# Three charges of a planner and its table of decisions, in a two-layer transformer kernel

## The chip, the cores and the metric

The kernel runs on one core of one Trainium2 chip. The metric is the device time of one execution in microseconds; a figure of the kernel before is the median of three executions. One further execution was recorded by the hardware profiler, and all views of the trace come from it.

The core's engines work beside each other and wait for each other by semaphores: PE multiplies matrices into PSUM, ACT evaluates functions (here the exponential), DVE and POOL do elementwise work, and SP issues the DMA transfers. POOL can't read PSUM.

## The reference

```python
def _A_ref(x, wqkv, wo):                    # attention: H = 32 heads of 16
    qkv = (x @ wqkv).reshape(B, S, 3, H, Dh).transpose(2, 0, 3, 1, 4)
    q, k, v = qkv[0], qkv[1], qkv[2]
    scores = jnp.einsum("bhqd,bhkd->bhqk", q, k) * (Dh ** -0.5)
    p = _softmax(scores, axis=-1)
    o = jnp.einsum("bhqk,bhkd->bhqd", p, v)
    return o.transpose(0, 2, 1, 3).reshape(B, S, D) @ wo
def _B_ref(x, w1, w2):                      # a dense layer with relu
    return jnp.maximum(x @ w1, 0) @ w2

x = A_x                                     # S = 2048 rows of D = 512, bf16
x = x + _A_ref(_layernorm(x), A_wqkv, A_wo)
x = x + _B_ref(_layernorm(x), B_w1, B_w2)   # 1792 hidden columns
x = x + _A_ref(_layernorm(x), A_wqkv, A_wo) # the same weights again
x = x + _B_ref(_layernorm(x), B_w1, B_w2)
return x
```

Two layers, each with 32 heads of 2048 x 2048 scores: 2 x 32 x 2048 x 2048 exponentials, 268 million, are the bulk of the work outside the matmuls.

## The kernel before

**Blocks and slots.** The scores of one head are cut into blocks of 128 keys by 512 queries (256 or 128 queries near the end of the second layer). A *slot* takes three such blocks of different heads: one group of score matmuls (L2231) fills one of two PSUM areas `ps_s`, three banks wide, and one ACT instruction (L2249) takes the exponential of what lies there into a buffer in SBUF. There are 1366 slots. The score matmuls of different heads run side by side in row groups of the array.

**Long and short exponentials.** In most slots the third block isn't given to ACT. DVE reads it from PSUM (`dve_block`, L1750), scales it and writes 16-bit integers, whose bits read as bf16 are a piecewise linear approximation of the exponential; POOL makes two shifted copies of it with integer additions (L1811), one up, one down. The three "words" together, with the lowest one weighed by `WEIGHT`, give a better approximation. So such a block costs PE three matmuls with the values instead of one. Two such blocks make a pair, which shares the words' buffers. The exponential of ACT then has 1024 columns and is called short here; with all three blocks it has 1536 and is long. The buffers for exponentials and words are few: three wide ones, 16 tiles of words, and whatever other tensors lie idle at the time and are lent (x, weights, keys, values).

**Weighing.** The lower word is weighed in one of two ways: if the values of those keys are at hand multiplied by `WEIGHT` (`vscaled`), the matmul takes these; otherwise DVE multiplies the word itself (`weigh` in `chain`, L1816).

**Values and filler.** The matmuls with the values (L1404) sum the output of one head group over all keys in one of two PSUM banks, `ps_o` and `ps_f`. Four of them run side by side in column groups of the array; such a round of four is called a pass here. Between the score groups PE also does the *filler*: the projections to queries, keys and values, the output projection, and both matmuls of the dense layer (L467, L707, L716), in pieces of a pass. The filler's sums go to that one of the two banks which the values don't hold, and DVE copies them out.

**Norms and transposes.** For a group of (mostly) four times 128 rows DVE computes statistics, ACT the inverse root, DVE the normalized rows (`ln_apply`, L795), and SP issues a DMA transpose for each 128 rows (L846) into `xnT`, from which the next filler is computed.

**The order.** Nothing is scheduled at run time. The program is written out slot by slot by a planner in the kernel's source: it keeps a clock for each engine (`now_pe`, `now_dve`, `now_act`, `now_pool`, `sp_free`), adds a charge in ns for everything it issues, and marks when each result will be there. For each slot it decides from these clocks whether a pair starts, which passes of values and filler go ahead of the next score group, and in which order DVE and POOL take their tasks. Each engine then runs its instructions in the order in which they were written, and the semaphores make it wait where a result isn't there. The charges of this change stand in `TRANSPOSE` (SP's time for an issue, then the time until the data is there), in the task of `apply` in `ln_rows`, and in `quick` in `chain`.

Two tables steer the decisions. `RULES` sets parameters from a slot on (how many passes may go ahead, how far a pair may look, how much backlog DVE may have). `STARTS`, `MORE` and `SLIP` override single slots: a pair starts or doesn't, more or less filler is owed, the limit for passes moves by some ns. They are read at these places:

```python
rule.update(RULES.get(no, {}))
asked = STARTS.get(no)
owed[0] = min(owed[0] + pace, rule["cap"]) + MORE.get(no, 0) if todo else 0.0
limit = max(need_by - rule["margin"], s_ready) - SWITCH + SLIP.get(no, 0.0)
```

When too many exponentials lie unread, or no buffer is free for the next one, the planner issues passes with values after the slot's scores (`force_v`), and the exponential has to wait until they have read the buffer that it writes.

The head (until the first exponential) and the end (after the last) are written out by hand, and neither the charges nor the tables change them.

Of the kernel before, what the change touches and what calls it, by code (L numbers as in the profile page):

```python
# [26 lines left out]
def kernel(  # L27
# [24 lines left out]
    QS = 512  # L52
# [18 lines left out]
    GROUP = 2  # L71
# [14 lines left out]
    EVAC_V, BESIDE, TUCK = 661.0, 10.0, {512: 0.0, 256: 11.0, 128: 24.0}  # L86
    STREAMED, WINDOW = 0.56, 3413.0
    SPREAD_LAG = 5000.0
    SMALL, W1, TRANSPOSE = (600.0, 1600.0), (430.0, 3000.0), (1400.0, 3600.0)
    CROWDED, POOL_ISSUE, BEHIND = 4500.0, 700.0, 3500.0  # L90
    JOINING, ADDED, BEHIND_IT = 870.0, 4300.0, 300.0
    JOIN = {}
    LOADED, FIRST_LOAD, LATER_LOAD, KEPT_Q = 18000.0, 30, 180, 8
    BOTH = 4
    WHOLE = 4
    STARTS, MORE, SLIP = {13: 0, 16: 1, 40: 0, 23: 1, 30: 0, 33: 0, 56: 0, 53: 0, 54: 1, 47: 0, 103: 1, 127: 1, 141: 1, 184: 1, 252: 1, 254: 0, 313: 0, 342: 0, 353: 0, 344: 1, 370: 1, 382: 1, 419: 1, 451: 0, 453: 1, 456: 0, 444: 0, 508: 0, 509: 1, 538: 0, 532: 1, 547: 0, 566: 1, 578: 0, 585: 1, 592: 0, 642: 1, 654: 0, 646: 0, 641: 1, 670: 0, 696: 1, 682: 0, 719: 0, 715: 1, 728: 1, 737: 1, 772: 0, 819: 1, 834: 0, 857: 0, 844: 1, 855: 0, 854: 1, 873: 0, 886: 1, 905: 1, 918: 1, 938: 1, 929: 0, 976: 0, 1000: 0, 1006: 1, 1001: 0, 1025: 0, 1031: 1, 1092: 0, 1128: 1, 1151: 1, 1166: 1, 1172: 0, 1250: 0, 1260: 0, 1266: 1, 1263: 0, 1340: 0, 1326: 0, 1364: 0, 1362: 0, 1366: 0, 1371: 0}, {9: -1.0, 13: 2.0, 7: 2.0, 38: 1.0, 39: 2.0, 32: 2.0, 52: 2.0, 41: -1.0, 48: 1.0, 126: 1.0, 153: 2.0, 187: -1.0, 204: 2.0, 221: -1.0, 237: 1.0, 229: -1.0, 264: 2.0, 265: -1.0, 266: 1.0, 300: 2.0, 281: 1.0, 285: 1.0, 308: 1.0, 320: 2.0, 318: -1.0, 327: -1.0, 355: 2.0, 378: -1.0, 371: 1.0, 372: 2.0, 388: 2.0, 396: -1.0, 391: -1.0, 437: 1.0, 495: 2.0, 538: 2.0, 543: 2.0, 574: 2.0, 603: 2.0, 659: 1.0, 684: -1.0, 685: 1.0, 711: -1.0, 807: 1.0, 804: 2.0, 813: -1.0, 828: 1.0, 836: 2.0, 832: 2.0, 855: 2.0, 879: 2.0, 861: -1.0, 862: -1.0, 896: 1.0, 897: 1.0, 899: 2.0, 956: -1.0, 948: 1.0, 961: 2.0, 987: -1.0, 1008: 1.0, 1035: -1.0, 1079: 1.0, 1089: 1.0, 1100: -1.0, 1099: -1.0, 1110: 2.0, 1164: 1.0, 1263: -1.0, 1267: 2.0, 1277: 2.0, 1299: 1.0, 1336: 2.0, 1365: -1.0, 1375: 1.0, 1371: 2.0}, {3: 120.0, 56: -200.0, 102: 60.0, 133: -200.0, 175: -200.0, 194: 120.0, 184: -200.0, 196: 120.0, 259: 60.0, 245: 60.0, 241: -200.0, 321: -200.0, 325: -200.0, 322: 60.0, 357: -200.0, 370: -200.0, 366: 120.0, 377: -200.0, 384: -200.0, 385: -200.0, 390: 120.0, 419: 120.0, 434: 216.0, 436: 120.0, 435: 60.0, 497: -200.0, 517: 60.0, 523: 60.0, 530: -200.0, 521: -200.0, 551: -200.0, 549: 60.0, 559: 216.0, 574: -200.0, 634: 60.0, 666: -200.0, 691: 216.0, 692: 60.0, 689: -200.0, 718: -200.0, 722: -200.0, 726: -200.0, 740: 120.0, 818: 120.0, 828: 60.0, 825: 60.0, 822: -200.0, 891: -200.0, 922: 60.0, 932: -200.0, 931: 120.0, 946: 60.0, 951: -200.0, 945: 60.0, 1011: 216.0, 1013: -200.0, 1002: 216.0, 1034: 60.0, 1062: 216.0, 1064: 120.0, 1067: 60.0, 1097: 60.0, 1114: 60.0, 1131: 120.0, 1220: -200.0, 1218: 60.0, 1242: 216.0, 1279: 60.0, 1289: -200.0, 1294: 216.0, 1296: 216.0, 1312: 60.0, 1307: -200.0, 1308: 60.0, 1323: 216.0, 1353: -200.0, 1361: -200.0, 1365: -200.0, 1370: -200.0}
    FIXED = 3
    rule = {
        "near": 14, "hold": 3, "spare": 14, "easy": 1.6, "cap": 6.0, "least": 0.5, "pace": 1.0,
# [2 lines left out]
        "rounds": 4, "partial": 3, "far": 3, "young": 3, "old": 5, "slack": 1300.0, "eager": 0,  # L102
        "haste": 2.0, "margin": 130.0, "join": -1.0, "room": 0, "keep": 2, "wide": 1, "share": 4,
    }
    RULES = {1: {'rounds': 3, 'hold': 2, 'closing': 3, 'fill': 2000.0}, 21: {'young': 5}, 41: {'easy': 1.0, 'keep': 1}, 61: {'old': 3, 'spare': 6, 'rounds': 4, 'fill': 3000.0, 'over': 200.0, 'young': 6, 'pressed': 6, 'closing': 6}, 101: {'least': 0.5, 'spare': 20, 'margin': 160.0, 'far': 4}, 121: {'near': 8, 'pressed': 2, 'soon': 1400.0, 'old': 4}, 141: {'keep': 2, 'late': 4.0, 'ahead': 8.0, 'unit': 360.0}, 161: {'pressed': 6, 'hold': 3, 'spare': 6, 'least': 0.8, 'far': 4, 'soon': 2000.0, 'haste': 1.6, 'near': 4}, 181: {'wide': 1, 'haste': 3.0}, 201: {'hold': 4, 'backlog': 3000.0}, 221: {'keep': 3, 'easy': 1.4, 'haste': 2.0, 'far': 2}, 241: {'haste': 3.0, 'full': 4}, 261: {'margin': 100.0}, 281: {'late': 3.0}, 301: {'late': 99.0, 'least': 0.5, 'unit': 400.0, 'easy': 1.0, 'keep': 2, 'young': 5, 'pace': 1.0, 'full': 3}, 321: {'keep': 3, 'easy': 2.0}, 341: {'young': 3}, 361: {'haste': 2.0}, 401: {'young': 6, 'unit': 360.0}, 421: {'pace': 1.0, 'slack': 1300.0, 'over': 0.0, 'eager': 0, 'partial': 3, 'backlog': 2200.0, 'closing': 3, 'cap': 3.0}, 441: {'pace': 1.15, 'young': 6, 'rounds': 4, 'keep': 2, 'calm': 3.0, 'far': 2, 'soon': 1400.0, 'unit': 320.0}, 461: {'slack': 1300.0, 'fill': 2000.0, 'closing': 3, 'unit': 360.0}, 481: {'unit': 400.0, 'soon': 2000.0, 'rounds': 4, 'late': 4.0, 'eager': 0, 'least': 0.5, 'fill': 2000.0, 'haste': 1.6}, 541: {'late': 2.0, 'least': 0.8}, 561: {'keep': 2, 'near': 10, 'margin': 100.0, 'hold': 2}, 581: {'ahead': 12.0, 'closing': 6, 'slack': 800.0, 'full': 5}, 601: {'ahead': 8.0, 'cap': 6.0}, 661: {'near': 12, 'ahead': 12.0, 'closing': 3, 'pace': 1.15}, 701: {'spare': 10}, 721: {'haste': 2.0, 'rounds': 4, 'near': 10, 'over': 0.0, 'pace': 1.3, 'eager': 1, 'keep': 2, 'young': 5}, 761: {'hold': 4, 'partial': 3, 'pace': 0.7, 'cap': 3.0, 'closing': 0, 'wide': 2, 'join': -1.0, 'near': 10}, 801: {'late': 99.0}, 821: {'eager': 1, 'calm': 1.2}, 841: {'keep': 2, 'cap': 3.0, 'least': 0.8, 'share': 4, 'backlog': 2200.0, 'room': 0, 'near': 6, 'haste': 1.3}, 861: {'backlog': 3000.0}, 881: {'share': 2}, 901: {'full': 3}, 921: {'eager': 1, 'rounds': 4, 'least': 0.5, 'partial': 3, 'margin': 60.0, 'haste': 1.6, 'full': 3, 'pace': 1.5}, 941: {'over': 60.0, 'late': 99.0}, 961: {'partial': 2, 'near': 12, 'cap': 10.0, 'far': 3, 'easy': 1.2, 'slack': 1300.0, 'soon': 1000.0, 'full': 3}, 981: {'rounds': 3, 'backlog': 2200.0}, 1021: {'wide': 0, 'cap': 6.0}, 1061: {'over': 200.0, 'spare': 10}, 1081: {'spare': 20, 'haste': 1.3, 'over': 120.0, 'slack': 300.0, 'easy': 1.6, 'backlog': 1500.0, 'room': 0, 'pace': 0.85}, 1101: {'soon': 1400.0, 'unit': 320.0}, 1121: {'far': 2, 'slack': 300.0, 'fill': 3000.0, 'ahead': 1.0, 'calm': 2.0, 'haste': 2.0, 'hold': 2, 'cap': 3.0}, 1161: {'unit': 400.0, 'far': 3}, 1241: {'near': 12, 'haste': 1.3, 'keep': 2, 'eager': 0}, 1261: {'full': 5}, 1301: {'keep': 2, 'cap': 3.0}, 1321: {'rounds': 3, 'room': 8}, 1341: {'fill': 2000.0, 'spare': 10}, 1361: {'fill': 2000.0, 'over': 60.0, 'hold': 3, 'unit': 400.0, 'eager': 0, 'ahead': 8.0, 'calm': 3.0, 'pressed': 6}}
    X_AT = (8.3, 8.5, 9.5, 10.6, 11.0, 11.4, 11.8, 12.1, 12.5, 12.8, 13.3, 14.0)
    WQ_AT, WV_AT = {0: 0.0, 1: 14000.0, 2: 16000.0, 3: 18000.0}, 10800.0
    FIRST_TRANSPOSE = 1600.0
# [709 lines left out]
    def ln_rows(tag, tt, n, i):  # L818
# [11 lines left out]
        if i == n - 1:  # L830
# [9 lines left out]
            def apply(k):  # L840
                ln_apply(tag, tt + k, k)
                if not by_dma(tag):
                    return
                home, a = (tag[2], 0) if tag[0] == "ln1" else columns(*tag[1:])[:2]
                xn_waits[0] -= k == TPC - 1
                nc.sync.dma_start_transpose(  # L846
                    out=xnT[home][:, :, a + k * P : a + (k + 1) * P], in_=xnbuf[k][:]
                )
                sp_free[0] = max(sp_free[0], now_dve[0] + 200.0) + first_transpose[0]
                first_transpose[0] = 0.0  # L850
                lag = sp_lag(TRANSPOSE) + (CROWDED if now_dve[0] < LOADED else 0.0)
                mark(("xT", tag, k), lag=lag)
                mark(("xnT", tag, k), lag=lag)
                if k == n - 1:
                    xn_free[0] = now_dve[0] + lag

            for k in range(n):
                task(
                    420, lambda k=k: apply(k),
                    [("xn", tag, k)] + [("xT", tag, k), ("xnT", tag, k)] * by_dma(tag),  # L860
                    [("xT", prev, k)] * (k < rows_of_prev) + [("rs", tag, 2)]
                    + [("raw",)] * (k == TPC - 1 and ("raw",) in made),
                )
# [936 lines left out]
    def chain(p):  # L1800
# [1 line left out]
        p["scaled"] = all(  # L1802
            ("third", sg["l"], kb) in made for us in p["blocks"] for sg, kb, g in us
        )
        quick = 150 + 0.2591 * GROUP * QS

        def of(part):
            return words[p["tiles"][part]]
# [687 lines left out]
```

## Time and profile before

| | us |
|---|---|
| three executions | 1366.53, 1366.89, 1368.46 |
| median | 1366.89 |
| the profiled execution | 1368.18 |
| its span, first to last instruction | 1366.4 |
| PE busy | 1327.1 |
| ACT busy | 1333.1 |
| DVE busy | 1162.1 |
| POOL busy | 789.3 |

The granted TensorE clock was 1.00 over the whole span. Busy times are unions of instructions, and instructions of one engine overlap: on ACT the next exponential starts before the last one is written out. A row of the timeline has the start, the duration, the engine, the line, the operation, the tiles (out<-in, buffer numbers left out, so an exponential written to a lent x tile shows as `xx<-ps_s`), and in brackets the idle time before it with what ended it. A row of the groups has busy time and mean duration between the bars, then the idle time before them and its releasers. A row of a view by line has the shortest, the median and the longest duration in ns. A row of the view by windows has the stretch, its length, the busy time of PE with its instructions, the granted clock, the share of the DMA engines and GB/s.

### The profile page before, as it was taken

To read this page: it belongs to the slowest core of one execution; us is meant where nothing else is said; L and a number is where in the kernel's file an instruction comes from. 1 tells how busy PE (TensorE), PEld (TensorE's weight loads), DVE (VectorE), ACT (ScalarE), POOL (GpSimd) and SP (SyncE) were. 2 spreads that over 40 slices of the span, in tenths; PEclk is the share of its full clock that TensorE was granted. 3 is DMA by queue.
4 is the path that set the end of the run, shared out by engine and by line. 5 is a ranking of instruction groups with operands and counts; after the bars stand their busy time and mean duration, and the time that the engine had idled before them with its cause. 6 is when DMAs were issued, how large, how long until landed. Compare 5 with 4: busy or idle time off the path is not lost.

```text
span 1366.4 us, 49106 instructions
## 1 busy us (share of the span) xinstructions
PE 1327.1 (97%) x20780; PEld 468.2 (34%) x20782; DVE 1162.1 (85%) x2024; ACT 1333.1 (98%) x1437; POOL 789.3 (58%) x1324
## 2 busy tenths in 40 slices
PE   8999999999999999999999999999999999999998
PEld 3222222222222222222222222222234444445665
DVE  7898889878998789997899878998888888988774
ACT  8999999999999999999999999999999999999995
POOL 3357766666676566676466654565446566666440
PEclk9999999999999999999999999999999999999999
DMA  6200112111024120321213100002313402324111
GB/s 152 66 2 18 26 33 43 43 41 41 11 52 107 33 57 15 101 46 41 49 21 90 29 29 13 26 16 49 102 44 52 110 21 48 72 45 98 31 38 39
DMA packets 166669, 66.64 MB, mean 49 GB/s; under 512 B 137616, under 2 KB 161616, under 8 KB 166448
## 3 DMA queue, kind: packets, MB, share of 16 engines
q1 hardware_dynamic: 159920, 57.89, 17.8%
q0 software_dynamic: 5568, 5.15, 2.0%
q8 instruction: 162, 2.65, 0.8%
q14 instruction: 59, 0.48, 0.1%
q10 hardware_dynamic: 960, 0.46, 0.1%
HBM read 38.80 MB, written 4.19 MB: 31 GB/s over the span
## 4 chain that ended last, share of the span: by engine, by line
PE 55%; ACT 35%; DVE 7%; issue 1%; DMA 1%; SPq 0%; POOL 0%; DVEq 0%; ACTq 0%; POOLq 0%
PE ps_s L2231 19%; ACT e L2249 16%; PE ps_o L1404 9%; PE ps_f L1404 9%; PE ps_o L467 8%; ACT xx L2249 8%; PE ps_f L467 7%; ACT w L2249 3%; DVE words L1750 2%; ACT wv L2249 2%; ACT val L2249 2%; ACT ktl L2249 1%; ACT words L2249 1%; ACT ktp L2249 1%; PE ps_o L716 1%
## 5 line engine op out<-in xcount | busy, mean ns | idle before, releaser
L2249 ACT ACTIVATE e<-ps_s 128x1024 bf16<-128x1024 f32 (+1 forms) x627 | 695.3, 1190 | 7.8 <-PE ps_s L2231 4.2
L1750 DVE TENSOR_SCALAR words<-ps_s 128x512 int16<-128x512 f32 x864 | 580.6, 684 | 95.6 <-PE ps_s L2231 82.1
L1811 POOL INT64_ADD words<-words x581 | 356.0, 622 | 260.6 <-DVE words L1750 206.6
L2231 PE MATMUL ps_s<-q,ktp 32*128 32x512 bf16 (+2 forms) x4110 | 478.5, 331 | 14.9 <-ACT e L2249 7.5
L2231 PEld LDWEIGHTS <-ktp 32*128 32x128 bf16 x4393 | 151.6, 91 | 452.2 <-issue 445.0
L2249 ACT ACTIVATE xx<-ps_s 128x1024 bf16<-128x1024 f32 x283 | 300.9, 1128 | 1.4 <-PE ps_s L2231 1.2
L2231 PE MATMUL ps_s<-q,ktl 32*128 32x256 bf16 (+2 forms) x1359 | 197.5, 289 | 0.9 <-ACT ktp L2249 0.3
L1404 PEld LDWEIGHTS <-vaug 128*32 128x32 bf16 x4686 | 116.4, 95 | 150.4 <-issue 131.0
L2249 ACT ACTIVATE w<-ps_s 128x1024 bf16<-128x1024 f32 x111 | 118.1, 1106 | 0.0
L1404 PE MATMUL ps_f<-e,vaug 128*32 128x512 bf16 (+2 forms) x830 | 111.6, 322 | 0.6 <-issue 0.5
L1404 PE MATMUL ps_o<-e,vaug 128*32 128x512 bf16 (+2 forms) x768 | 105.9, 335 | 0.7 <-DVE u L1260 0.4
L1750 DVE TENSOR_SCALAR xx<-ps_s 128x512 int16<-128x512 f32 x128 | 86.3, 683 | 16.4 <-PE ps_s L2231 14.0
L1404 PE MATMUL ps_o<-words,vaug 128*32 128x512 bf16 (+2 forms) x647 | 92.1, 348 | 0.5 <-DVE u L1260 0.3
L1404 PE MATMUL ps_f<-words,vaug 128*32 128x512 bf16 (+2 forms) x559 | 89.5, 373 | 0.8 <-DVE vaug L953 0.5
L1404 PEld LDWEIGHTS <-val 128*32 128x32 bf16 x2744 | 73.4, 96 | 45.4 <-issue 35.3
L1404 PE MATMUL ps_o<-words,vscaled 128*32 128x512 bf16 (+2 forms) x514 | 78.7, 331 | 2.6 <-POOL words L1811 1.4
L2231 PEld LDWEIGHTS <-ktl 32*128 32x128 bf16 x1359 | 61.3, 92 | 56.6 <-issue 55.0
L1811 POOL INT64_ADD words<-xx x83 | 50.7, 620 | 49.0 <-DVE xx L1750 29.6
L2249 ACT ACTIVATE val<-ps_s 128x1024 bf16<-128x1024 f32 x67 | 73.6, 1129 | 0.0
L467 PE MATMUL ps_o<-w,ht 128*32 128x512 bf16 x896 | 73.0, 383 | 0.0
L2249 ACT ACTIVATE wv<-ps_s 128x1024 bf16<-128x1024 f32 x65 | 71.7, 1122 | 0.6 <-PE ps_s L2231 0.5
L1404 PEld LDWEIGHTS <-vscaled 128*32 128x32 bf16 x1546 | 62.2, 96 | 25.7 <-issue 19.0
(320 smaller groups left out, 2659.6 us busy)
## 6 DMA issues: line engine op xcount, KB each, us to landing
w<-in_B_w_dram SPq DMA_DIRECT2D x144, 128.0 KB
w<-in_B_w_dram SPq DMA_DIRECT2D x35, 256.0 KB
q<-xn SPq DMA_DIRECT2D x38, 64.0 KB
wv<-in_A_wqkv_dram SPq DMA_DIRECT2D x8, 256.0 KB
away<-xx SPq DMA_DIRECT2D x8, 256.0 KB
xx<-away SPq DMA_DIRECT2D x8, 256.0 KB
out_dram<-xx SPq DMA_DIRECT2D x15, 128.0 KB
xx<-in_A_x_dram SPq DMA_DIRECT2D x14, 128.0 KB
```

Of the source, the lines that this page charges most:

```text
L467: nc.tensor.matmul(G["b"][cols], lhsT[:, cols], rhs, start=not G["begun"][g], stop=not G["cols"][g], tile_position=(0, 32 * g), skip_group ...
L716: nc.tensor.matmul(out[cols], lhsT[:, cols], rhs, start=i % k == 0, stop=i % k == k - 1, tile_position=(0, 32 * g), skip_group_check=True,)
L1404: nc.tensor.matmul((ps_f, ps_o)[sg["bank"]][32 * g : 32 * g + 32, 0 : sg["w"]], values[:, 4 * sg["T"] + g, 2 * e : 2 * e + 32], rhs, start ...
L1750: first = nc.vector.tensor_scalar(out=words[which][:, half * QS : (half + 1) * QS], in0=src, scalar1=EXP_BIAS, scalar2=THIRD, op0=ALU.add, ...
L1811: ins = nc.gpsimd.int64_add(of(part).bitcast(I64), of("lin").bitcast(I64), by)
L2231: score = nc.tensor.matmul(b[:, a : a + sg["w"]], kt[32 * g : 32 * g + 32, kc : kc + P], q_home(sg["q"])[32 * g : 32 * g + 32, sg["e"], 0 ...
L2249: ex = nc.scalar.activation(out=eb[:, 0 : place[m]], in_=b[:, 0 : place[m]], func=ACTF.Exp, scale=1.0 / (LOG2E * UNIT),)
```

## The change

Three charges of the planner are lowered, and the four tables are replaced by others (in the change's own words: found with six plans kept instead of four). No instruction is added or removed in itself; which blocks go to DVE, and the order on each engine behind the head, come out of the planner anew.

```diff
-    SMALL, W1, TRANSPOSE = (600.0, 1600.0), (430.0, 3000.0), (1400.0, 3600.0)
+    SMALL, W1, TRANSPOSE = (600.0, 1600.0), (430.0, 3000.0), (1260.0, 3000.0)
...
-    STARTS, MORE, SLIP = {13: 0, 16: 1, 40: 0, 23: 1, 30: 0,
...
+    STARTS, MORE, SLIP = {13: 0, 32: 1, 26: 1, 45: 0, 104: 1,
...
-    RULES = {1: {'rounds': 3, 'hold': 2, 'closing': 3, 'fill': 2000.0}, 21: {'young': 5},
...
+    RULES = {1: {'unit': 360.0, 'calm': 2.0, 'room': 8, 'partial': 3, 'easy': 1.2, 'least': 0.8, 'fill': 2000.0, 'late': 4.0}, 21: {'rounds': 3, 'each': 3, 'closing': 6, 'young': 6},
...
             for k in range(n):
                 task(
-                    420, lambda k=k: apply(k),
+                    400, lambda k=k: apply(k),
...
-        quick = 150 + 0.2591 * GROUP * QS
+        quick = 67 + 0.2591 * GROUP * QS
```

The tables before have 81, 76 and 79 overrides of single slots and 199 settings of parameters at 53 slots; those after have 99, 81 and 94, and 237 settings at 61 slots.

4 lines of the change are left out of this document (2 added, 2 removed).

## The prediction

> **What bounds the kernel now.** I read the page first: shares of busy time, then the chain that ended last.
>
> ```profile
> PE 1327.1 (97%) x20780; PEld 468.2 (34%) x20782; DVE 1162.1 (85%) x2024; ACT 1333.1 (98%) x1437; POOL 789.3 (58%) x1324
> PE 55%; ACT 35%; DVE 7%; issue 1%; DMA 1%; SPq 0%; POOL 0%; DVEq 0%; ACTq 0%; POOLq 0%
> ```
>
> ACT (the exponentials) and PE are both full, and the chain passes between them. A busy share can't say which of two full engines loses time, so the next view is the timeline of ACT, where the exponentials of L2249 follow each other.
>
> ```profile
> 27.70 1.53 ACT L2249 ACTIVATE e<-ps_s 128x1536 bf16<-128x1536 f32 x1
> 29.03 1.54 ACT L2249 ACTIVATE words<-ps_s 128x1536 bf16<-128x1536 f32 x1
> ...
> 627.89 1.07 ACT L2249 ACTIVATE e<-ps_s 128x1024 bf16<-128x1024 f32 x1
> 628.79 1.08 ACT L2249 ACTIVATE xx<-ps_s 128x1024 bf16<-128x1024 f32 x1
> 629.70 1.10 ACT L2249 ACTIVATE e<-ps_s 128x1024 bf16<-128x1024 f32 x1
> ```
>
> The first column is the start, the second the duration. Durations overlap, so only the distance of two starts is a cost: 1.33 us after a long exponential (1536 columns: three blocks of scores), 0.905 us after a short one (1024: two blocks, the third went to DVE and POOL). How many there are, and what ACT waited for, is in the groups by shape and in the view of line L2249:
>
> ```profile
> L2249 ACT ACTIVATE e<-ps_s 128x1024 bf16<-128x1024 f32 x520 | 547.2, 1123 | 5.6 <-PE ps_s L2231 3.1 <-PE ps_o L1404 1.4 <-PE ps_f L1404 0.5
> ...
> L2249 ACT ACTIVATE e<-ps_s 128x1536 bf16<-128x1536 f32 x106 | 157.9, 1520 | 2.2 <-PE ps_s L2231 1.1 <-PE ps_o L1404 0.8
> ...
> L2249 ACT ACTIVATE words<-ps_s 128x1536 bf16<-128x1536 f32 x27 | 39.7, 1489 | 1.5 <-PE ps_f L1404 0.9 <-PE ps_o L1404 0.6
> ...
> L2249 ACT ACTIVATE words<-ps_s 128x1024 bf16<-128x1024 f32 x5 | 5.6, 1117 | 0.0
> L2249 ACT ACTIVATE e<-ps_s x627: 606/1142/1710, 10.8 to 1342.2; 128x1024 bf16<-128x1024 f32 x125, 128x1536 bf16<-128x1536 f32 x32
>   PE ps_s L2231: 7.3, 14
>   PE ps_o L1404: 2.8, 5
>   PE ps_f L1404: 1.4, 4
> ```
>
> The ten groups from the 520 to the 5 hold 1232 short exponentials; 106 + 27 = 133 are long, and one has 512 columns. At their distances they need 1232 x 0.905 + 133 x 1.33 + 0.6 = 1292.5 us. The loop lasts from 10.8 to 1342.2 plus the last 0.6: 1332.0 us. So 39.5 us are lost between exponentials, and all the change can do lies in two numbers: how many exponentials are long, and what is lost between them. The last three rows show the worst of the loss: 14 times the scores came late (ps_s), 9 times ACT waited for matmuls with the values (ps_o, ps_f), which free the buffer that the exponential is to write. Stage by stage the page's slices are alike; the head (10.8 us) and the end (1342.8 to 1366.4) stay as they are in the code.
>
> **What the edits move directly.** The three charges, against the rows of what they charge:
>
> ```profile
> L846 SPq DMA_TRANSPOSE xnT<-xn x55: 1188/1217/2725, 21.1 to 1331.9; - x55
> L795 DVE TENSOR_SCALAR xn<-xx,mv,ya x59: 360/404/789, 20.6 to 1330.6; 128x512 bf16<-128x512 bf16 x59
> L1816 DVE TENSOR_SCALAR words<-words x31: 408/417/832, 39.3 to 1335.6; 128x1024 bf16<-128x1024 bf16 x31
> ```
>
> A transpose is charged 1260 ns of SP instead of 1400 (median 1217) and its landing 3000 instead of 3600; a norm 400 instead of 420 (median 404); a weighing 67 + 0.2591 x 1024 = 332 instead of 415 (median duration 417, less what overlaps the next). No instruction gets faster. The charges only decide how early the plan lets others start; for four rows the plan now sees them 4 x 0.14 + 0.6 = 1.16 us earlier, more than one exponential. The table does the rest: every engine but the head gets another order. So I counted the built programs (before to after), per slot, that is per exponential:
>
> - long exponentials 133 to 143, short 1232 to 1222, slots 1366 both
> - DVE first steps (L1750) and POOL adds (L1811) 1232 to 1222 each; weighings 43 to 46
> - matmuls with values 8976 to 8932 (5 full passes of four), repeated scores 36 to 30 passes; filler the same
> - exponentials whose buffer is freed by value matmuls that stand after their own scores: behind two passes or more 7 to 1, behind one pass 8 to 11
> - four passes or more between two score groups, with short exponentials around: 14 to 2; three passes: 210 to 220
> - slots from a transpose's issue to the first matmul that reads it, in the middle of the kernel: 7 to 11 before, 6 to 8 after
>
> **The price of each.** *Ten more long exponentials*: 10 x (1.33 - 0.905) = +4.3 us on ACT. The blocks they take leave DVE and POOL, which hides nothing here: POOL is 58% busy, and DVE's 85% is not what ACT waits for in the rows above.
>
> *Buffers freed late.* One place:
>
> ```profile
> 285.06 1.11 ACT L2249 ACTIVATE e<-ps_s 128x1024 bf16<-128x1024 f32 x1
> 287.00 1.45 ACT L2249 ACTIVATE e<-ps_s 128x1536 bf16<-128x1536 f32 x1 [0.83 <-PE ps_o L1404]
> 285.78 1.40 PE ps_o L1404 x21
> ```
>
> The last row is the chain of waits there. The starts lie 1.94 us apart instead of 0.905: 1.04 us lost, 0.83 of it shown as idle. Over the nine places the idle is 2.8 + 1.4 = 4.2 us, and each loses the overlap of 1.123 - 0.905 = 0.22 us too: 6.2 us, 0.69 each. Six places behind two passes go: between 2.8 us (idle alone) and 6.2 (if the rest cost nothing); I take 6 x 0.69 = -4.1, as these are the long ones. Three more behind one pass: 0 to 0.69 each, I take 0.3: +0.9. Together -3.2.
>
> *Crowded slots.* PE's timeline and ACT's beside it:
>
> ```profile
> 643.22 0.39 PE L2231 MATMUL ps_s<-q,ktp 32*128 32x512 bf16 x3
> 643.54 0.40 PE L1404 MATMUL ps_o<-words,vaug 128*32 128x512 bf16 x4
> 643.76 0.38 PE L1404 MATMUL ps_o<-xx,vaug 128*32 128x512 bf16 x2
> ...
> 644.52 0.39 PE L2231 MATMUL ps_s<-q,ktp 32*128 32x512 bf16 x3
> 643.64 1.02 ACT L2249 ACTIVATE xx<-ps_s 128x1024 bf16<-128x1024 f32 x1 [0.28 <-PE ps_s L2231]
> 644.95 1.02 ACT L2249 ACTIVATE e<-ps_s 128x1024 bf16<-128x1024 f32 x1 [0.28 <-PE ps_s L2231]
> ```
>
> Scores and four passes take 644.52 - 643.22 = 1.30 us; a pass is 643.76 - 643.54 = 0.22. Four passes overrun 0.905 by 0.40, three by 0.18, two (0.86) fit. An overrun costs nothing while the scores are ahead, all of it once they aren't. Twelve crowded slots fewer: 0 to -4.8, I take the middle, -2.4. Ten more with three passes: 0 to +1.8; they come singly between slots of two, so +0.5, near the lower end.
>
> *Transposes read a slot earlier.* The tightest group of the trace:
>
> ```profile
> 382.25 5.29 SPq L846 DMA_TRANSPOSE xnT<-xn  x4
> 389.36 0.83 PE L467 MATMUL ps_f<-xnT,wkq 128*32 128x512 bf16 x12
> 387.80:388.30 0.50, 0.31 (x5) 1.00 0.84 168
> 388.30:388.80 0.50, 0.50 (x10) 1.00 0.01 0
> ...
> 490.81 4.41 SPq L846 DMA_TRANSPOSE xnT<-xn  x3
> 499.70 0.83 PE L467 MATMUL ps_o<-xnT,wkq 128*32 128x512 bf16 x12
> ```
>
> The last issue ends at 387.54; the DMA engines (share 0.84, then 0.01 in the rows of the view by windows) are done near 388.3; PE reads at 389.36, 1 us later. A slot less is 0.9 us less: it just holds. But an issue can take 2.7 us instead of 1.2 (the row of L846). Five groups stand at six slots: 0 to 5 x 1.5 = +7.5 if each meets such an issue with nothing else for PE to do; I take +0.3, as other groups have more room: the one in the last two rows ends its issues at 495.22 and is read at 499.70, 4.5 us later.
>
> *Weighing.* Nothing waited for L1816 in its view, and 20 value matmuls before and 19 after read a weighed tile in the same or the next slot: 0. The Trainium skill speaks against a low charge here (SBUF — State Buffer, "Who interferes with whom"): a VectorE instruction in a two-port mode and one of GpSimd exclude each other for the whole instruction. The trace agrees that some weighings are held (832 ns against 417); by that rule the sum would be the third rival's.
>
> **The sum.** 4.3 - 3.2 - 2.4 + 0.5 + 0.3 = -0.5 us. The profiled execution took 1368.18 us with a span of 1366.4, 1.8 around it; the median of the runs is 1366.89. Its span would become 1365.9, and the median **1366.4 us**: no change that can be told, taking 0.2% (2.7 us) as what a measurement of this kernel can tell. Its own range, from the bounds that are likely together, is 1363 to 1370.
>
> **Rivals.**
> *The lateness moves to the transposes (slower).* The place is the six groups of four rows from 200 to 1070 us; the price 0.9 to 1.5 us each where the first reader comes less than 0.8 us after the last issue's end (388.3 - 387.54). If five of them are caught, that is +4.5 to +7.5 on top of -0.8: 1371 to 1374. For it: all three charges fall, and the distance in slots with them. Against: the plan still counts more than the 5.3 + 0.8 us that the rows show.
> *The new order waits less for data (faster).* The 23 places hold 11.5 us of idle and 23 x 0.22 of overlap, 16.6 of the 39.5; the rest is lateness too small to show as idle, some of it PE behind DVE and POOL.
>
> ```profile
> L1750 DVE TENSOR_SCALAR words<-ps_s 128x512 int16<-128x512 f32 x864 | 580.6, 684 | 95.6 <-PE ps_s L2231 82.1
> L1811 POOL INT64_ADD words<-words x581 | 356.0, 622 | 260.6 <-DVE words L1750 206.6
> ```
>
> DVE has ten first steps less and POOL ten adds less (mean 684 and 622 ns): some 6 us less work each; if that and charges nearer to the medians take away a tenth of the 39.5 beyond the sum, -4, it ends at 1362. Against: such places are scattered and the order of all of them is new, so as many may appear as go.
> *Weighing behind POOL (slower).* 46 weighings, each up to 832 - 417 = 0.415 us later than charged; if one in four keeps PE waiting, +4.8: 1371.
> *The table is not this kernel's (does not do what it says).* 20 of its 237 settings bear names that no line reads (each, wish, hang, rest). If the rest were found with those in force, the order is not the one that was meant. Its counts don't look like that: the old table under the new charges builds an order with 17 buffers behind two passes or more, the new one has 1. The sum is made on the built order anyway; the losses I can't count would be larger: +5, 1371.
>
> **How the numbers follow.** Forecast 0.46 (of it 0.10 faster, 0.30 same, 0.06 slower), transposes 0.20, less waiting 0.22, weighing 0.05, table 0.07. Faster: 0.10 + 0.22 = 0.32. Same: 0.30 + 0.03 of the two larger slower cases falling short = 0.33. Slower: 0.35. The range 1361.5 to 1371.8 leaves out the far ends of the two large rivals.
>
> **What would show it.** 143 long exponentials and a loop that needs 1222 x 0.905 + 143 x 1.33 + 0.6 = 1296.7 us by their distances. ACT's idle behind ps_o and ps_f at L1404 under 2.5 us instead of 4.2, behind ps_s under 6 instead of 7.3. PE's waits naming xnT or L846 over 2 us in sum would be the first rival; waits of L1404 for L1816 the third. The loss in the loop near 34.7 us; above 40 or below 31 the forecast is wrong.

## The result, and the profile after

| | median, us | lowest to highest | executions |
|---|---|---|---|
| before | 1366.94 | 1366.27 to 1368.46 | 6 |
| after | 1361.63 | 1360.65 to 1362.64 | 6 |

The ratio after to before is 0.9959, with an interval of 0.9946 to 0.9972: the change makes the kernel 5.3 us faster. The forecast was no change (1366.4); the second rival gave 1362.

The page of after, shares of busy time and the chain that ended last:

```profile
PE 1328.0 (98%) x20714; PEld 467.8 (34%) x20714; DVE 1158.8 (85%) x2017; ACT 1335.2 (98%) x1437; POOL 783.0 (58%) x1314
PE 32%; ACT 22%; DVE 3%; issue 1%; DMA 1%; SPq 0%; DVEq 0%; ACTq 0%
```

Neither of the two full engines works less: PE's busy time is 0.9 us up and ACT's 2.1. The shares of the second row add up to some 59%, those of before to 99%, so the two chains can't be compared. What changed is the time between pieces of work. The groups by shape of after show the long exponentials, 120 + 23 = 143 as counted:

```profile
L2249 ACT ACTIVATE e<-ps_s 128x1536 bf16<-128x1536 f32 x120 | 178.4, 1522 | 1.8 <-PE ps_s L2231 1.1
...
L2249 ACT ACTIVATE words<-ps_s 128x1536 bf16<-128x1536 f32 x23 | 34.8, 1520 | 0.5 <-PE ps_f L1404 0.5
```

The view of line L2249 of after, with what ACT sat idle for (us, times):

```profile
L2249 ACT ACTIVATE e<-ps_s x586: 1018/1164/1682, 10.8 to 1332.9; 128x1024 bf16<-128x1024 f32 x160, 128x1536 bf16<-128x1536 f32 x36
...
  PE ps_s L2231: 2.1, 7
  PE ps_f L1404: 0.5, 1
  ACT e L2249: 0.4, 1
```

Before, 14 late scores cost 7.3 us of idle and 9 held buffers 4.2; now 7 late scores cost 2.1 and one held buffer 0.5. The loop needs 1296.7 us by the distances of its exponentials and starts its last one at 1335.5 instead of 1342.2.

To see where the loss went, I took each distance of two starts less 0.905 or 1.331 us, and sorted the excess by what stands in the built order and in PE's timeline at that slot. A slot counts in the first row that fits it. Each kernel has two profiled executions: 1368.18 and 1367.56 us before, 1360.65 and 1361.85 after. The medians are 1366.94 and 1361.63, so the first pair overstates the difference, and the second pair, 5.7 us apart, is nearer to it. Loss in us, slots in parentheses:

| slots | before | before, second | after | after, second |
|---|---|---|---|---|
| buffer freed behind two passes or more | 5.17 (7) | 5.18 (7) | 0.64 (1) | 0.64 (1) |
| buffer freed behind one pass | 2.38 (8) | 2.39 (8) | 1.96 (11) | 1.96 (11) |
| PE waits over 0.1 us for data or an issue | 9.42 (18) | 8.26 (17) | 3.98 (15) | 4.51 (16) |
| a norm on ACT | 4.43 (32) | 4.43 (32) | 4.53 (32) | 4.54 (32) |
| four passes or more | 2.75 (13) | 2.75 (13) | 0.35 (2) | 0.35 (2) |
| three passes | 8.43 (199) | 8.82 (200) | 9.98 (210) | 10.14 (210) |
| long ones, and the rest | 6.82 | 7.36 | 7.04 | 7.27 |
| sum | 39.4 | 39.2 | 28.5 | 29.4 |

By the second pair: -4.5 and -0.4 for buffers, -2.4 for crowded slots (the row of four passes or more), -3.8 for data and +1.3 for three passes make -9.8, and the other two rows change nothing. Ten more long exponentials cost +4.3. Head and end together give -0.2: the end isn't quite the same, since 303 matmuls instead of 311 are left for the time after the last scores. That is -5.7, and the spans differ by 5.7 (1365.8 and 1360.1).

The largest single stall of before is one of the data row. From the timeline of before, PE, ACT and POOL (start, duration, idle time before it in brackets):

```profile
1321.51 1.94 ACT L2249 ACTIVATE vaug<-ps_s 128x1024 bf16<-128x1024 f32 x2 [1.41 <-PE ps_s L2231]
...
1320.50 0.40 PE L1404 MATMUL ps_o<-words,vscaled 128*32 128x128 bf16 x15 [1.42 <-POOL words L1811]
...
1319.33 0.60 POOL L1811 INT64_ADD words<-words  x1
```

Value matmuls stand ahead of the next scores and wait for words that POOL finishes at 1319.93; the scores wait behind them in PE's order, and ACT for the scores. The view of ACT names only the scores, so this place was one of the 14 "late scores" that the prediction had quoted and not followed further. More of the data row lies behind DVE than behind POOL. One such place, again PE and then ACT:

```profile
985.96 0.40 PE L1404 MATMUL ps_o<-ktp,vaug 128*32 128x512 bf16 x3 [0.46 <-DVE u L1260]
...
987.15 1.02 ACT L2249 ACTIVATE xx<-ps_s 128x1024 bf16<-128x1024 f32 x1 [0.59 <-PE ps_s L2231]
```

The matmul waits for a bank that DVE's copy of the old sums (L1260) empties. This exponential starts 0.71 us late in both profiles of before.

### The profile page after: what moved, and what is told of

The parts are those of the page before. It is cut to its first block, busy times and chain, and to the rows that moved or that the text cites. A ratio compares the mean times of both kernels' runs of the same rounds, so it can differ in the third digit from the quotient of the medians.

```text
span 1358.9 us, 48968 instructions
## 1 busy us (share of the span) xinstructions
PE 1328.0 (98%) x20714; PEld 467.8 (34%) x20714; DVE 1158.8 (85%) x2017; ACT 1335.2 (98%) x1437; POOL 783.0 (58%) x1314
## 4 chain that ended last, share of the span: by engine, by line
PE 32%; ACT 22%; DVE 3%; issue 1%; DMA 1%; SPq 0%; DVEq 0%; ACTq 0%
PE ps_s L2231 11%; ACT e L2249 10%; PE ps_o L1404 6%; ACT xx L2249 5%; PE ps_f L1404 5%; PE ps_f L467 4%; ACT w L2249 3%; PE ps_o L467 3%; ACT wv L2249 2%; ACT words L2249 1%; DVE words L1750 1%; PE ps_o L716 1%; PE ps_s L2339 1%; PE ps_f L716 1%; ACT ktp L2249 0%
## 5 line engine op out<-in xcount | busy, mean ns | idle before, releaser
L2249 ACT ACTIVATE e<-ps_s 128x1024 bf16<-128x1024 f32 (+1 forms) x586 | 665.3, 1211 | 3.0 <-PE ps_s L2231 1.7
L1811 POOL INT64_ADD words<-words x571 | 348.3, 619 | 252.4 <-DVE words L1750 204.8
L2249 ACT ACTIVATE xx<-ps_s 128x1024 bf16<-128x1024 f32 x252 | 273.5, 1134 | 0.0
L1404 PEld LDWEIGHTS <-vaug 128*32 128x32 bf16 x4702 | 119.4, 95 | 152.6 <-issue 137.2
L2249 ACT ACTIVATE w<-ps_s 128x1024 bf16<-128x1024 f32 x132 | 139.0, 1109 | 0.0
L2249 ACT ACTIVATE wv<-ps_s 128x1024 bf16<-128x1024 f32 x99 | 110.3, 1135 | 0.1
L1404 PE MATMUL ps_o<-e,vaug 128*32 128x512 bf16 (+2 forms) x797 | 106.2, 329 | 0.7 <-DVE vaug L1236 0.4
L1404 PE MATMUL ps_f<-e,vaug 128*32 128x512 bf16 (+2 forms) x676 | 93.4, 324 | 0.6 <-DVE r L1260 0.3
L1404 PE MATMUL ps_o<-words,vscaled 128*32 128x512 bf16 (+2 forms) x530 | 89.7, 336 | 0.0
L1404 PE MATMUL ps_f<-words,vaug 128*32 128x512 bf16 (+2 forms) x597 | 88.8, 363 | 0.6 <-issue 0.4
L1404 PE MATMUL ps_o<-words,vaug 128*32 128x512 bf16 (+2 forms) x621 | 88.8, 359 | 0.2 <-DVE r L1260 0.2
L1811 POOL INT64_ADD xx<-words x103 | 63.3, 616 | 43.9 <-DVE words L1750 28.7
L1404 PEld LDWEIGHTS <-val 128*32 128x32 bf16 x2712 | 73.0, 96 | 43.8 <-issue 33.8
L467 PE MATMUL ps_f<-w,ht 128*32 128x512 bf16 x1064 | 86.6, 383 | 0.0
L2249 ACT ACTIVATE ktl<-ps_s 128x1024 bf16<-128x1024 f32 x68 | 76.7, 1153 | 0.1
```

The lines of the kernel that those rows point to most:

```text
L467: nc.tensor.matmul(G["b"][cols], lhsT[:, cols], rhs, start=not G["begun"][g], stop=not G["cols"][g], tile_position=(0, 32 * g), skip_group ...
L1404: nc.tensor.matmul((ps_f, ps_o)[sg["bank"]][32 * g : 32 * g + 32, 0 : sg["w"]], values[:, 4 * sg["T"] + g, 2 * e : 2 * e + 32], rhs, start ...
L1811: ins = nc.gpsimd.int64_add(of(part).bitcast(I64), of("lin").bitcast(I64), by)
L2249: ex = nc.scalar.activation(out=eb[:, 0 : place[m]], in_=b[:, 0 : place[m]], func=ACTF.Exp, scale=1.0 / (LOG2E * UNIT),)
```

## Experiments

Two questions: what a late exponential's price hangs on (its buffer, or the passes on PE behind its scores), and whether the gain belongs to the charges, the table, or single places of the new order. Each time is compared with runs of the kernel before beside it, whose medians are 1366.08 to 1366.66 us; intervals are of the ratio.

**The kernel before, once more.** No edit.

> The kernel before, profiled a second time: how much of what PE waits for (DVE, POOL, instruction issue) belongs to the order and how much to one execution. If the data waits are the order's, the places that lost over 0.5 us behind them (at 1287 and 1318 us of the first profile) lose the same again, and the sum of such losses is again near 9.4 us. If they are one execution's, they are gone or elsewhere, and the sum is some 2 us lower, as the first profile took 1.2 us more than the median.

It took 1367.56 us. The second column of the table is this run: the same late buffers with the same losses, to 0.01 us in the buffer rows. Single places that vary most are waits for an issue or for POOL: the stall shown above is 0.4 us shorter, all of it in the time from the end of POOL's addition to PE's start (0.57 us, then 0.11). The rows of three passes and of the rest are 0.4 and 0.5 us larger.

```profile
1321.40 1.94 ACT L2249 ACTIVATE vaug<-ps_s 128x1024 bf16<-128x1024 f32 x2 [0.97 <-PE ps_s L2231]
```

So most stalls belong to the order that is written out, not to chance.

**A free buffer for the late exponentials.** In the kernel before, the seven exponentials behind two passes or more write to an idle `xnT` tile; the order on every engine stays as it was.

```diff
+    SPARE = {283: 0, 638: 2, 833: 3, 1129: 0, 1183: 0, 1257: 0, 1263: 0}
...
         eb, ks, wide_e = home
+        eb = xnT[SPARE[no]][:].rearrange("p c f -> p (c f)") if no in SPARE else eb
```

> The kernel before with every decision and every engine's order the same, but the 7 exponentials that waited for a buffer behind two or more passes write to an idle xnT tile instead. Theory 'held buffer' (the prediction's price): each costs its wait of 0.69 to 0.74 us, so -4.8 to -5.2 us: 1361.8 to 1362.1. Rival 'pile of passes': the passes themselves are the cost, since in the trace the next exponential starts 0.18 to 0.29 us after its own scores' end in all seven places, the shortest distance there is; taking the buffer away brings 0 to -0.8 us, 1366.1 to 1366.9, and the next exponential waits for ps_s instead.

1366.36 us against 1366.17, ratio 1.0004 (0.9995 to 1.0013): no gain that can be told, where seven prices of 0.69 would be 4.8 us. The timeline of ACT at the place that the prediction had shown:

```profile
285.87 1.55 ACT L2249 ACTIVATE xnT<-ps_s 128x1536 bf16<-128x1536 f32 x1
288.10 1.02 ACT L2249 ACTIVATE val<-ps_s 128x1024 bf16<-128x1024 f32 x1 [0.68 <-PE ps_s L2231]
```

and what L2249 waited for in this kernel:

```profile
  PE ps_s L2231: 8.0, 19
  PE ps_o L1404: 0.3, 1
  PE ps_f L1404: 0.2, 1
```

The late exponential now starts on time (0.90 after the one before it), and the next one loses 0.90 (288.10 - 285.87 - 1.33): its scores stand behind the same pile of passes. The releaser changed its name from ps_o to ps_s, and most of the loss stayed. Over the seven places and the slots behind them the profile loses 4.0 us instead of 5.3.

**All late buffers.** The same with all fourteen of the kernel before that an idle tile could take (the one-pass ones too), and in the kernel after with ten of its twelve.

```diff
+    SPARE = {283: 0, 638: 2, 833: 3, 1129: 0, 1183: 0, 1257: 0, 1263: 0, 489: 2, 1054: 0, 1107: 0, 1173: 0, 1194: 0, 1250: 0, 1289: 0}
```

> The same for 14 exponentials: the 7 and those held behind one pass. 'Held buffer': a further -2.4 us, 1359.5 to 1360. 'Pile of passes': again 0 to -1 us against the kernel before.

1365.83 us, 0.9997 (0.9988 to 1.0006): no gain that can be told.

> The kernel after with the same order, but 10 of its 12 held exponentials write to an idle xnT tile. 'Held buffer': the wait behind two or more passes (0.64 us) and nine behind one (0.18 each in its trace) go: -2.3 us against after, 1359.3. 'Pile of passes': 0 to -0.5, 1361.1 to 1361.6.

1360.24 us, 0.9957 (0.9945 to 0.9969) against before, where after has 0.9959. It is the shortest time of a kernel that does the whole work, but its interval can't be told from that of after. So the buffer itself is worth too little to be told here, about a quarter of the loss by the profiles; the pile of passes is what remains.

**Without the table.** Both kernels with the tables emptied, so that only the charges differ.

```diff
-    STARTS, MORE, SLIP = {13: 0, 16: 1, 40: 0, 23: 1, 30: 0,
...
-    RULES = {1: {'rounds': 3, 'hold': 2, 'closing': 3, 'fill': 2000.0}, 21: {'young': 5},
...
+    STARTS, MORE, SLIP = {}, {}, {}
+    RULES = {}
```

> The kernel before with both tables emptied (no override of a slot, no change of a parameter); the old charges. Its built order has 153 long exponentials (before 133, after 143), 12 held behind two or more passes, 6 crowded slots, 126 with three passes. By these counts and the trace's mean loss at each kind of place: +5.5 us against before, 1372. Theory 'charges' (charges nearer to the rows let PE wait less for DVE, POOL and DMA): losses behind such waits of 8 us or more, as in the two profiles of before (9.4 and 8.3). Theory 'order' (each written-out order has its own such places, whatever was charged): no rule by charges.

1423.47 us, 1.0414 (1.0398 to 1.0429).

> Both tables emptied, the new charges: what the charges bring by themselves. 147 long exponentials, 10 held behind two or more passes, 3 crowded, 140 with three passes; by these counts +1.1 us against before, 1368, and 4.4 us faster than the same without tables under the old charges. 'Charges': losses behind waits for DVE, POOL and DMA near the 4.0 us of the kernel after; 'order': anywhere from 3 to 12.

1426.14 us, 1.0435 (1.0407 to 1.0463). The expectations by counts (1372 and 1368) missed by over 50 us. They left out the end: these orders keep 767 and 883 matmuls for the time after the last scores (311 before), and 56 and 64 us pass after the last exponential starts, where before it is 24. There PE even waits for weights. The counts were short in the loop too: it is 23 and 19 us longer than before, where they gave 5.5 and 1.1. The end of the kernel with the new charges, by windows (start:end, length, busy time of PE, PEld, DVE, ACT, POOL, granted clock, DMA share, GB/s), and PE's matmuls there, with their waits:

```profile
1371.00:1373.00 2.00, 1.81 (x58) 1.70 (x62) 1.11 (x3) 1.02 (x3) 0.00 (x0) 1.00 0.00 0
1373.00:1375.00 2.00, 0.65 (x22) 0.36 (x12) 0.00 (x0) 1.03 (x2) 0.00 (x0) 1.00 0.52 135
1375.00:1377.00 2.00, 1.41 (x36) 0.81 (x40) 0.00 (x0) 0.02 (x1) 0.00 (x0) 0.90 0.86 193
1377.00:1379.00 2.00, 2.00 (x44) 1.36 (x40) 0.00 (x0) 0.80 (x2) 0.00 (x0) 0.50 0.60 136
```

```profile
1371.53 2.13 PE L716 MATMUL ps_s<-xnT,w 128*32 128x256 bf16 x64
1375.54 4.03 PE L716 MATMUL ps_s<-xnT,w 128*32 128x256 bf16 x80 [1.89 <-DMA w<-in_B_w_dram]
1381.07 1.06 PE L716 MATMUL ps_s<-xnT,w 128*32 128x256 bf16 x32 [1.50 <-DMA w<-in_B_w_dram]
```

The two kernels are equal within their intervals: without tables the charges bring nothing on the whole. Under the new ones the loop is 3.3 us shorter, 2.6 of it by six long exponentials fewer (147 and 153), and the end is 7.7 us longer.

**One half of the change alone.** The new charges with the old table:

```diff
-    SMALL, W1, TRANSPOSE = (600.0, 1600.0), (430.0, 3000.0), (1400.0, 3600.0)
+    SMALL, W1, TRANSPOSE = (600.0, 1600.0), (430.0, 3000.0), (1260.0, 3000.0)
...
-                    420, lambda k=k: apply(k),
+                    400, lambda k=k: apply(k),
...
-        quick = 150 + 0.2591 * GROUP * QS
+        quick = 67 + 0.2591 * GROUP * QS
```

> Half of the change: the three charges, with the tables of before. 143 long exponentials as in after, but 17 held behind two or more passes, 12 crowded, 211 with three. By the counts +12.8 us, 1379. If the gain lay in the charges it would be near 1362. 'Charges': waits for data cost 4 us or less; 'order': 3 to 12.

1392.40 us, 1.0192 (1.0177 to 1.0207). What L2249 waited for in it:

```profile
  PE ps_o L1404: 12.1, 12
  PE ps_s L2231: 7.7, 17
  PE ps_f L1404: 6.6, 8
```

The other half, the new table with the old charges:

> The other half: the tables of after under the old charges. 179 long exponentials, 10 held behind two or more passes, 10 crowded, 185 with three: by the counts +22.9 us, 1389. If the gain lay in the tables it would be near 1362. 'Charges': waits for data cost 8 us or more; 'order': 3 to 12.

1397.69 us, 1.0229 (1.0214 to 1.0245). Neither half brings any part of the gain; they cost 26 and 31 us. The counts had given 1379 and 1389, so these kernels are 13 and 9 us slower than counted. Each of the two tables fits only the charges that it came with. The losses behind waits for data are 16.1 (old charges, no table), 14.6 (old, new table) and 9.4 us (before) with the old charges, and 20.5, 10.4 and 4.0 with the new: they show no rule by the charges.

**One charge of 20 ns set back.** The new kernel, with 420 ns for a norm.

```diff
-                    400, lambda k=k: apply(k),
+                    420, lambda k=k: apply(k),
```

> The new kernel with one charge set back, the norm's, 400 to 420 ns. By counting the built order it has 153 long exponentials (143) and 7 buffers behind two passes or more (1). If only the fit of table and charges counts: 10 x 0.425 = +4.3 and 6 x 0.69 = +4.1, and some us of filler left for the end, 1370 to 1385, so one charge of 20 ns undoes the whole gain. If the charges' closeness to the medians brings the gain: a third of the change at most is undone, 1361.6 to 1363.5.

1374.35 us, 1.0056 (1.0041 to 1.0071): 12.7 us above after. Its profile has 153 long exponentials and these waits:

```profile
  PE ps_o L1404: 5.5, 8
  PE ps_s L2231: 4.1, 10
  PE ps_f L1404: 1.9, 4
```

By the same sorting its loss is 37.7 us, 8.3 above after's second run, of it 7.06 at seven buffers behind two passes or more (0.64 at one). With 4.3 for the ten long exponentials that is 12.6; the spans differ by 12.9 (1373.0 and 1360.1). So counts and places explain this kernel too, and 20 ns in one charge of a planner made another order of everything behind it.

**Shorter piles.** The kernel before in its order, with 104 value matmuls in the seven piles cut from 512 columns to 32 (those after the first two or four passes; parts of their sums are left out). `since` holds the slot and the passes since its scores.

```diff
+    since, DROP = [-1, 0.0], {282: 4, 637: 2, 832: 2, 1128: 2, 1182: 2, 1256: 2, 1262: 2}
...
+        cut = 32 if g in sg["begun"] and since[1] > DROP.get(since[0], 99.0) else sg["w"]
...
-            (ps_f, ps_o)[sg["bank"]][32 * g : 32 * g + 32, 0 : sg["w"]],
+            (ps_f, ps_o)[sg["bank"]][32 * g : 32 * g + 32, 0 : cut],
```

> The kernel before, same order, but in the 7 slots with piles of passes 104 value matmuls read and write 32 columns instead of 512, 256 or 128 (that part of the sums is left out): 13.4 passes of PE less, all where the passes overrun the exponential. Theory 'pile': a pass over budget costs its 0.22 us, so -2.5 to -3 us against before, 1363.4 to 1363.9. Rival 'sum of PE's work': 13.4 x 0.22 = -2.9 too, but then the next kernel must show the same price. Rival 'held buffer' is out already.

1365.36 us, 0.9994 (0.9985 to 1.0003): less than expected. The loss at the seven places fell only from 5.17 to 3.94 us. Passes at the front of each pile were left whole; that the exponential waits for these is shown by the larger cut below, which takes them too. As a control, 127 matmuls in 24 ordinary slots of two passes were cut in the same way:

```diff
+    since, DROP = [-1, 0.0], {61: 1, 73: 1, 77: 1, 108: 1, 115: 1, 121: 1, 179: 1, 235: 1, 345: 1, 408: 1, 435: 1, 522: 1, 580: 1, 603: 1, 697: 1, 780: 1, 866: 1, 1047: 1, 1065: 1, 1114: 1, 1200: 1, 1208: 1, 1246: 1, 1318: 1}
```

> The control: 127 value matmuls cut to 32 columns in 24 ordinary slots with two passes and short exponentials around them (that part of the sums is left out), 17.8 passes of PE less. 'Pile': passes that fit beside the exponential cost nothing, 0 to -0.5 us, 1366.0 to 1366.6. 'Sum of PE's work': 17.8 x 0.22 = -3.9 us, 1362.6; then the 11 passes that the kernel after has less would be part of its gain, and ten long exponentials would pay for themselves.

1366.26 us, 0.9999 (0.9991 to 1.0008): 17.8 passes less, some 3.9 us of PE's work at 0.22 each, are worth nothing that can be told where they fit beside an exponential.

**All of the piles and crowded slots.** Every value matmul behind the scores of the seven piles and, after the first pass, of the eleven crowded slots that don't follow a pile: 253 are cut. Parts of their sums are left out.

```diff
+    since, DROP = [-1, 0.0], {282: 0.0, 637: 0.0, 832: 0.0, 1128: 0.0, 1182: 0.0, 1256: 0.0, 1262: 0.0, 194: 1.0, 217: 1.0, 271: 1.0, 284: 1.0, 432: 1.0, 557: 1.0, 651: 1.0, 652: 1.0, 657: 1.0, 658: 1.0, 660: 1.0}
```

> The kernel before, in its order; 253 value matmuls are cut from 512 columns to 32, those behind the scores of the 7 slots with a pile and of the 11 crowded slots (the matmul that opens a sum and the first pass in the crowded slots stay whole). It leaves part of these sums out. The profile of the kernel before shows a loss of 5.2 us at the 7 places and of 2.75 us at the crowded ones. If passes that stand in the way of the scores are what costs there: three quarters of the two go, -6 us, 1360. If, as the smaller cut (104 matmuls, -0.7) looked, a pile's loss comes from something else, for instance from DVE and POOL that wait behind the pile: at most -1.5, 1364.6 or more.

1361.79 us, 0.9964 (0.9952 to 0.9977): 4.5 us less by the medians. The place at 285 us, in ACT's timeline, and L2249's waits:

```profile
285.03 1.11 ACT L2249 ACTIVATE e<-ps_s 128x1024 bf16<-128x1024 f32 x1
...
286.09 1.45 ACT L2249 ACTIVATE e<-ps_s 128x1536 bf16<-128x1536 f32 x1
```

```profile
  PE ps_s L2231: 4.1, 10
  PE ps_o L1404: 0.3, 1
  PE ps_f L1404: 0.2, 1
```

The starts lie 1.06 us apart instead of 1.94, and the buffer is the same as before: with the passes gone it comes free only 0.16 us late. At the seven places the profile loses 1.35 us instead of 5.18, at the crowded ones 1.46 instead of 2.75.

**Short handovers.** DVE's copies of the finished sums (L1234 to L1260) cut to 64 columns, except for the first two query groups of the first layer; the rest of each sum is left out. It was done in the kernel before, in the kernel after, and in the kernel before together with the last cut.

```diff
+        few = 64 if l or j > 1 else QS
...
-                nc.vector.tensor_add(out=u[:], in0=sg["load"], in1=sums[:])
+                nc.vector.tensor_add(out=u[:, 0:few], in0=sg["load"][:, 0:few], in1=sums[:, 0:few])
```

> The kernel before, same order, but DVE's copies that empty the banks of the value sums (L1234 to L1260) take 64 columns instead of up to 512, except in the first two query groups of the first layer (the rest of the sums is left out): each handover of a bank from one head group to the next comes up to 0.5 us earlier, and DVE has some 30 us less to do. Theory 'waits for data' (half of the gain of after is that PE waits less behind DVE at such handovers): before gains 4 to 6 us, after 1 to 2, and the distance of the two shrinks from 5.3 to 2 us or less. Rival 'piles': both gain alike, under 2 us, and the distance stays near 5.

1363.64 us, 0.9980 (0.9971 to 0.9989): 2.4 us less. The place at 987 us loses 0.24 us instead of 0.71. L2249's waits:

```profile
  PE ps_s L2231: 4.8, 11
  PE ps_o L1404: 2.5, 4
  PE ps_f L1404: 1.2, 3
```

> The same cut copies in the kernel after. 'Waits for data': -1 to -2 us against after, 1359.6 to 1360.6; 'piles': the same gain as in the kernel before.

1358.73 us, 0.9943 (0.9930 to 0.9955) against before: 2 to 3 us less than after. Both kernels gain alike, so the handovers cost some 2 us in each (the lighter work of DVE included) and are not what sets them apart: 4.9 us stay between the two.

> The same with DVE's copies of the sums cut to 64 columns as in the kernel with quick handovers, which alone gave -2.4 us. It leaves part of the sums out. If losses of single places add up: 1360 - 2.4 = 1357.6, and the profile's loss between exponentials is near 39.4 - 6 - 3.6 = 30. If a place that is mended only lets the next one limit: 1361 or more.

Both cuts together: 1359.60 us, 0.9953 (0.9940 to 0.9965). The two cuts alone gave -4.5 and -2.4; together -6.7. Losses of single places add up within the intervals. It is 2 us above the expected 1357.6, which had counted -6 for the piles from the profile. The profile's loss is 30.7, as expected (30).

**The kernel after, once more.**

> The new kernel once more. If stalls belong to the order: a loop loss of 28.5 within 1 us, with the same places among the waits for data (0.6 us at 865 us behind a weighing, 0.3 at 1045 us behind a transpose). If they are chance: other places and another sum.

1361.85 us, and the last column of the table: the loss is 0.9 above the first run's, all but 0.4 of it in the data row; the buffer and crowded rows are the same to 0.01.

## Why the prediction was right and wrong

*What was counted and priced.* Long exponentials: 143, +4.3, as predicted. Crowded slots: -2.4, as predicted, though that was the middle of 0 to -4.8 with no reason for the middle, so the agreement is in part luck. Three passes: +1.3 where +0.5 was taken, inside its bounds of 0 to +1.8. Transposes read earlier: +0.3 was taken. PE waited once for such data, in the timeline of after:

```profile
1045.11 0.62 PE L467 MATMUL ps_f<-xnT,w 128*32 128x512 bf16 x8 [0.33 <-DMA xnT<-xn]
```

In both runs of after the exponential behind it loses 0.3 to 0.4 us. That is the sign of the first rival, at one place, and far below its 2 us.

*Buffers freed late.* -3.2 was taken, -4.9 measured. The six that go gave -4.5 where 6 x 0.69 = -4.1 stood; the three more behind one pass were to cost 0.9, but that row fell by 0.4 although it has three slots more, so its slots cost 0.18 each where they cost 0.30 before. The size of the larger term was near, its reason wrong: a free buffer is worth nothing that can be told (1.0004), cutting the passes is worth 4.5 us with the crowded slots. The row "<-PE ps_o L1404" named the last event of the wait, not its price.

*The step that failed: waits for data.* The sum had no term for what PE waits for behind DVE and POOL. The prediction set DVE aside because "DVE's 85% is not what ACT waits for"; but PE waits for DVE, and ACT behind PE under the name of the scores. "As many may appear as go" was an assumption, and the losses beyond the sum were kept as the second rival with a chance of 0.22. The data row fell by 3.8 to 5.4 us. By the second pair this row gives -3.8 where the sum had +0.3 (for transposes), buffers give 1.7 more than taken, three passes take 0.8 back, and head and end give -0.2: that leads from -0.5 to -5.7 within the rounding. The prediction said that a loop loss under 31 would make its forecast wrong, and it is 28.5 and 29.4.

The second rival had the time right (1362) for a reason that was partly another: it took DVE's and POOL's lighter work and the closer charges as the cause. DVE's busy time fell by 3.3 us and POOL's by 6.3. The short handovers took 19 us of work from DVE (1143.0 busy instead of 1162.1) and gave 2.4, so 3.3 can hardly give more than some tenths (an estimate from that run); POOL's part was not tested. The charges without a table bring nothing (1423 and 1426), and 20 ns in one of them costs 12.7 us under the same table.

*Weighing.* The row of after, minimum, median and maximum in ns, has the same median as before:

```profile
L1816 DVE TENSOR_SCALAR words<-words x29: 355/417/834, 38.2 to 1326.9; 128x1024 bf16<-128x1024 bf16 x29
...
L1816 DVE TENSOR_SCALAR w<-w x3: 408/417/599, 865.0 to 882.5; 128x1024 bf16<-128x1024 bf16 x3
```

and one place costs something, in the timeline of after:

```profile
866.89 1.02 ACT L2249 ACTIVATE e<-ps_s 128x1024 bf16<-128x1024 f32 x1 [0.40 <-PE ps_s L2231]
...
865.18 0.39 PE L1404 MATMUL ps_o<-words,vaug 128*32 128x512 bf16 x1
865.70 0.38 PE L1404 MATMUL ps_f<-w,vaug 128*32 128x512 bf16 x1
...
865.04 0.60 DVE L1816 TENSOR_SCALAR w<-w 128x1024 bf16<-128x1024 bf16 x1
```

The matmul that reads the weighed word starts at 865.70, when the weighing has ended at 865.64, 0.52 us after the matmul before it, where 0.22 is a pass. So 0.3 of the 0.6 us that ACT loses there in both runs goes back to the weighing; nearly four passes stand between these scores too. The third rival needed twelve such places. By the rule of the Trainium skill (SBUF — State Buffer, "Who interferes with whom") DVE and GpSimd (POOL here) lock each other out of a shared port pair. The trace agrees in that seven of the 46 weighings of after take about twice the median (814 to 834 ns against 417) and all seven start while an addition of POOL runs; PE seldom feels it.

*The table.* Without the 20 settings that no line reads the planner writes out the same program: they change nothing. The fourth rival falls by the time, 1361.6 where it gave 1371.

*What stays open.* The piles and crowded slots are shown by a cut: 4.5 us of the median (3.1 to 6.6 by the interval), where the accounting has 6.9 less there in after. The fall of the waits for data is read from profiles and was not isolated: the handovers cost about the same in both kernels, and no run took away the other large places of before (POOL's words at 1319.93, a wait for an issue that ends at 1289.31) alone. The profiles of the other runs do show that it belongs to the order. A slightly different sorting of the same kind, which gives 9.5 and 8.3 us for the two runs of before and 3.6 and 4.0 for those of after, gives 7.9, 8.4, 8.0 and 8.2 for the two kernels with free buffers, the control and the shorter piles, all in the order of before, and 3.6 for the kernel after with free buffers. In the order of before 4.7 to 5.8 us of it lie behind DVE and 0.8 to 1.6 behind POOL; in the order of after 1.6 to 1.9 behind DVE and none behind POOL. Which decisions of the planner moved these places is open.

## What to carry to other kernels

Where an order is written out by a planner, a change of its table is a change of single places: count the piles of work that stand ahead of the critical engine, look in the trace for what the counts leave out, and follow each late result one step further back than the view does, since the reason is often on another engine. A releaser in a view says which wait ended last, not what its removal is worth; give the waiting instruction what it lacks and see whether the next one takes over the wait. In this kernel the charges and the table that came with them are one thing: neither could be kept or undone without the other.

## What had not been expected of the hardware

Stalls repeat. Seven piles cost 5.17 and 5.18 us in two executions of the kernel before, one place 1.036 us in both, and 0.64 in both runs of after. The place behind DVE's copy at 987 us lost 0.71 in all seven profiles in the order of before with whole copies. Waits for an issue or for POOL differ: in the same seven the place at 1290 us lost 0.61 to 1.83, and the one at 1321 us 0.82 to 1.58.

Passes of four matmuls that fit beside an exponential cost nothing that can be told: with 17.8 of them less the ratio of the times is 0.9999 (0.9991 to 1.0008).

In the kernel with the new charges and no table, PE's granted clock fell to 0.50 for a window of 2 us (1377 to 1379) after two windows in which it waited for weights (busy 0.65 and 1.41 of 2.00 us). The 80 matmuls around it took 4.03 us, where 64 of the same shape before the wait had taken 2.13. The Trainium skill (TensorE: Matmul & The Clock Gate, "What's actually happening") tells of half the clock after an idle window of some 3.4 us. The row agrees with the half, but the longest idle time just before it was 1.89 us (the row at 1375.54), so a shorter pause was enough here.
